# Linear attention with RMS norm and a mish FFN on one core: every engine in source order by slots, k^T v of all batches made in the first tile, q in whole rows

## The chip, the core and the metric

The kernel runs on one core of a Trainium2 chip. The metric is the device time of one execution in microseconds, lower is better. The core has a matrix engine (TensorE, PE in the profile), a vector engine (VectorE, DVE), a scalar engine (ScalarE, ACT), a general one (GpSimd, POOL) and a queue that issues transfers (SyncE, SP). Each works through its own list of instructions in order and waits on semaphores for the others; sixteen DMA engines move data between DRAM and the on-chip memory.

## The reference

Inputs are q, k, v of 8 batches, 8 heads, 576 tokens and 64 channels, a gain g of 64 channels, and two weight matrices, which arrive as 64-bit floats.

```python
kv = einsum('bhsd,bhse->bhde', k, v)          # 64x64 per batch and head
out = einsum('bhsd,bhde->bhse', q, kv)
rms = sqrt(mean(out * out, axis=-1, keepdims=True) + 1e-06)
x = (out / rms * g).transpose(0, 2, 1, 3).reshape(4608, 512)
h = x @ w_in                                  # 512 -> 2048
sp = where(h > 20, h, log1p(exp(minimum(h, 20))))
result = (h * tanh(sp)) @ w_out               # mish, 2048 -> 512
```

## The kernel before

The 4608 tokens are cut into nine tiles of 512. A tile crosses from one batch to the next (`segments`), since a batch has 576 tokens.

**Precision and Strassen.** Both large matmuls run on operands split in two (`split`: ACT rounds a copy to fp32r as the high half, DVE subtracts it to get the low half), and each product is three matmuls of halves. Each matmul is cut into 2x2 blocks by the Winograd form of Strassen's scheme: seven products (`PROD`) of sums of blocks, called A11, S1, S2, S4, A12, S3, A22 on the side of the tokens and T1 to T4, B11, B21, B22 on the side of the weights. The weights, 64-bit in DRAM, are first turned into 32-bit floats by a scaling on ACT and three integer operations on DVE (`join`), and then into the seven forms (`weight_forms`: `differences`, `first`, `rest`).

**The first stage** (tiles 0 to 8) makes h and mish(h) and stores them in DRAM (`gd`). Per tile four groups `n` of seven products run, each product 12 matmuls of 256 columns; this is a *slot*, so a tile is `NS` = 28 slots. Results are moved out of the accumulation banks by copies on ACT and additions on DVE (`group`, `put_in`), then mish runs on ACT. The bank "a" takes up A11, S2, S3 and, in the next group, A22; "bc" takes S1 with S4, and A12.

**Attention** for tile j is made during tile j-1, in two units of four heads (`unit_steps`): `load` of q in rows of 32 channels (128 bytes), `transpose` on DVE, `project` (k^T v times q on PE), `square` on ACT, `sums` (a matmul with a matrix of ones, which leaves the sum of squares on all rows of a head), `rstd` (a table load, Ln and Exp on ACT) and `normalize` on DVE. Tiles 0 and 1 use plain fp32, the others split halves. k^T v of batch j is made during tile j-1 as well: four loads (`kv_load`, two heads each, four DMAs, L206 and L207) and four products (`kv_product`, L242), which are copied into two block-diagonal tiles of halves, kvh and kvl. Then the seven forms of x are made (`x_sums`, `x_form`).

During tiles 1 to 8 the forms of w_out are made, 16 blocks one after the other, and stored in DRAM (`wod`).

**The second stage** multiplies mish(h) by w_out in 18 blocks of 256 tokens. The first is interleaved with the arrival of the weights (L673), the others run seven products of 24 matmuls each (L605).

**What sets the order.** A table `plan` holds for each slot what is recorded behind its product (`at`, `trace`). Only SP works in the order of the source (`manual_schedule(engines={SP})`); the instructions of PE, DVE, ACT and POOL are ordered by a scheduler that plans their times. The stores of gd are issued from ACT's queue.

Of the kernel before, what the change touches and what calls it, by code (L numbers as in the profile page):

```python
# [16 lines left out]


START = "w0 k0 q0 k1 q1 w1 c0 m0 t0 s0 m1 r0 t1 s1 c1 r1 w2 a0 f0 f1 a1 f2 f3 f4 f5 w3"


# [4 lines left out]
PROD = ((A11, B11, "a"), (S1, T1, "c"), (A22, T4, "p"), (S2, T2, "a"), (S4, B22, "c"), (A12, B21, "b"), (S3, T3, "a"))  # L26
# [3 lines left out]
def linear_attention_rms_mish_ffn(  # L30
# [26 lines left out]

    nc = tc.nc
# [4 lines left out]
    P = 128  # L63
    T = 512
# [5 lines left out]
    NQ = NF2 // 2  # L70
    G = 2 * P
# [10 lines left out]
    fp = ctx.enter_context(tc.tile_pool(name="fp", bufs=5))  # L82
# [5 lines left out]
    kvp = part1.enter_context(tc.tile_pool(name="kvp", bufs=1))  # L88
    xp = part1.enter_context(tc.tile_pool(name="xp", bufs=1))
    wst = part1.enter_context(ExitStack())  # L90
    wpools = {}

    def weight_pools(raw, x, forms):

        wst.close()
        for name, bufs in (("w64", raw), ("wx", x), ("wst", forms)):
            if bufs:
                wpools[name] = wst.enter_context(tc.tile_pool(name=name, bufs=bufs, reuse_waits="tile"))

    gcol = const.tile([P, 1], F32, name="gcol")  # L100
    ones = const.tile([P, P], F32R, name="ones")
    eps = const.tile([P, 1], F32, name="eps")
    gd = [tc.dram_tile([P, NFC, T], F32, name=f"gd{i}") for i in range(NT)]
    wod = [tc.dram_tile([P, 7, 2, G], F32, name=f"wod{c}") for c in range(NF2)]


    last = []

    def in_turn(i):
        if last:  # L110
            order = mybir.DependencyInfo(mybir.DependencyClass.NoSync, mybir.DependencyReason.DATA)
            tc.add_manual_dep(i.ins, last.pop().ins.name, order, reason="tables")
        last.append(i)

    def mish(o, i):
        in_turn(nc.scalar.activation(o, i, AF.Mish))  # L116
# [9 lines left out]
    def weight_forms(srcs, m, n, forms, put=None):  # L126
# [4 lines left out]
        def load():  # L131
            t = wpools["w64"].tile([P, 4, w, 2], U32, name="w64")
            n_ = 4 // len(srcs)
            for i, src in enumerate(srcs):
                dst = t[:, i].rearrange("p (m n) t -> p m (n t)", m=m) if n_ == 1 else t[:, n_ * i:n_ * i + n_].rearrange("p b n t -> p b (n t)")
                nc.sync.dma_start(dst, src)  # L136
            st["w"] = t.rearrange("p b n t -> p (b n) t")

        def scale():
            st["x"] = (wpools["wx"] if put else att).tile([P, 4 * w], F32, name="wx" if put else "fl")  # L140
# [9 lines left out]
        def differences():  # L150
            x = st["x"].rearrange("p (b n) -> p b n", b=4)
            d = st["w"].rearrange("p n t -> p (n t)").bitcast(F32)[:, 0:4 * w].rearrange("p (b n) -> p b n", b=4)
# [4 lines left out]
            st["f"] = forms()  # L157

        def parts(f0, f1, src):
            hi, lo = (st["f"][:, f0:f1, s].rearrange("p f m n -> p f (m n)") for s in range(2))  # L160
            split(hi, lo, src)

        def first():
            parts(T1, T4 + 1, st["d"])

        def rest():
            parts(B11, B11 + 1, st["x"][:, 0:1])
            parts(B21, B22 + 1, st["x"][:, 2:4])

# [3 lines left out]
        return load, scale, join, differences, first, rest, store  # L173
# [3 lines left out]
    def weight_in(j):  # L177
# [8 lines left out]
        return weight_forms(srcs, 2, P, forms)  # L186

    def weight_out(c, h):
        def forms():
            return wpools["wst"].tile([P, 7, 2, 1, P], F32R, name="wst")  # L190
# [7 lines left out]
        return weight_forms(srcs, 1, P, forms, store)  # L198


    def kv_load(b, h0, n, tiles):
        ts = []
        hs = slice(h0, h0 + n)
        for src in (k, v):
            m, r = tiles.pop(0), tiles.pop(0)
            nc.sync.dma_start(m, src[b, hs, 0:SM, :].rearrange("h (p c) d -> p h (c d)", c=CM))  # L206
            nc.sync.dma_start(r, src[b, hs, SM:S, :].rearrange("h p d -> p h d"))  # L207
# [3 lines left out]
    def kv_staging():  # L211
        ts = []
        for name in ("k", "v"):
            ts.append(kvp.tile([P, 2, CM * D], F32, name=f"{name}m"))
            ts.append(kvp.tile([SL, 2, D], F32, name=f"{name}r"))
        return ts

    kvf, kvh, kvl = {}, {}, {}  # L220

    def kv_new(b):
        def new(name, dtype):
            t = kvs.tile([P, NKC, P], dtype, name=name)
            nc.gpsimd.memset(t.bitcast(F32), 0.0)
            return t
        if b < T32:
            kvf[b] = new(("kvh0", "kvl0")[b], F32)
        if b >= T32 - 1:
            first = b < T32 + 1  # L230
            kvh[b] = new(f"kvh{b % 2}", F32R) if first else kvh[b - 2]
            kvl[b] = new(f"kvl{b % 2}", F32R) if first else kvl[b - 2]

    def kv_product(b, h0, nh, km, kr, vm, vr):
        ps = ps_t.tile([P, nh // 2, D], F32, name="s2")
        for i in range(nh // 2):
            for c in range(CM + 1):
                for o in range(2):
# [3 lines left out]
                    nc.tensor.matmul(ps[o * D:(o + 1) * D, i, :], kt, vt, start=(c == 0), stop=(c == CM))  # L242
        n = slice(h0 // 2, (h0 + nh) // 2)
        for r in (slice(0, D), slice(D, P)):
            if b < T32:
                nc.scalar.copy(kvf[b][r, n, r], ps[r, :, :])
            if b < T32 - 1:
                continue
            hi, lo = kvh[b][r, n, r], kvl[b][r, n, r]
            nc.scalar.copy(hi, ps[r, :, :])  # L250
            nc.vector.tensor_sub(lo, ps[r, :, :], hi.bitcast(F32))
# [11 lines left out]

    def unit_steps(j, u):
        st = {}

        def load(n):
            if n == 0:
                st["q"] = att.tile([P, 2, T], F32, name=f"qs{u}")
# [486 lines left out]
```

## Time and profile before

| | us |
|---|---|
| median of 3 runs | 930.96 |
| lowest, highest | 924.14, 932.98 |
| the profiled execution | 938.03 |
| its span, first to last instruction | 936.2 |

All views are of the profiled execution. Busy times are sums over an engine's instructions; a wait is put down to the instruction that ended it. "SPq" and "ACTq" are the queues that issue transfers. "PEclk" is the clock that TensorE was granted, 1.00 being full speed. The boundaries between tiles are taken from the first copy that follows a tile's first product (L374).

### The profile page before, as it was taken

How to read it: one execution, taken by the hardware profiler on the slowest of the kernel's cores; microseconds unless marked ns; L12 is line 12 of the kernel's file. 1: busy time of each engine (PE TensorE's matmuls, PEld its weight loads, DVE VectorE, ACT ScalarE, POOL GpSimd, SP SyncE). 2: the span in 40 equal slices, each digit the busy share in tenths (PEclk: the TensorE clock that was granted, in tenths of full speed). 3: DMA queues.
4: the chain of work that ended last, by engine and by line, in shares of the span. 5: the costliest groups of instructions: out<-in, count | busy, mean ns of one | idle time of the engine just before them, and what ended most of it. 6: DMA issues, size and time to landing. Idle time of an engine off the chain costs nothing.

```text
span 936.2 us, 17021 instructions
## 1 busy us (share of the span) xinstructions
PE 849.1 (91%) x6940; PEld 816.1 (87%) x6940; DVE 597.0 (64%) x832; ACT 512.8 (55%) x776; POOL 3.6 (0%) x14
## 2 busy tenths in 40 slices
PE   2687799898996998979899899999999999999997
PEld 1376699798896988969899898999999999999997
DVE  3676785665656557465753827767777767776661
ACT  2564767677676667666766744444444444444441
POOL 1000000000000000000000000000000000000000
PEclk9887889999897998999999999999999999999999
DMA  8565566676767667677741899443333443433421
GB/s 185 160 155 158 150 191 189 179 221 164 225 196 200 180 164 224 173 203 206 195 139 66 288 398 419 144 146 114 135 113 116 164 148 114 135 113 113 158 68 46
DMA packets 218861, 160.50 MB, mean 171 GB/s; under 512 B 91808, under 2 KB 208544, under 8 KB 217760
## 3 DMA queue, kind: packets, MB, share of 16 engines
q1 hardware_dynamic: 194016, 121.67, 44.3%
q10 hardware_dynamic: 24768, 37.76, 11.5%
q8 instruction: 54, 0.88, 0.4%
q14 instruction: 23, 0.19, 0.1%
HBM read 97.52 MB, written 61.87 MB: 170 GB/s over the span
## 4 chain that ended last, share of the span: by engine, by line
PE 70%; DMA 12%; SPq 6%; ACT 6%; DVE 3%; issue 2%; ACTq 0%; DVEq 0%
PE a L605 21%; PE bc L605 16%; PE a L411 16%; PE bc L411 11%; DMA w<-in_moe_w_out_dram 5%; SPq L274 3%; DMA w<-in_moe_w_in_dram 2%; SPq L136 2%; PE s L242 2%; PE q L673 2%; DMA qs<-in_q_dram 1%; DMA wod<-wst 1%; ACT L116 1%; ACT gf L119 1%; PE x L302 1%
## 5 line engine op out<-in xcount | busy, mean ns | idle before, releaser
L411 PE MATMUL a<-gf,wf 128*128 128x256 f32 x1728 | 248.1, 297 | 38.7 <-ACT ulb L116 22.3
L411 PEld LDWEIGHTS a<-gf,wf 128*128 128x128 f32 x1728 | 231.2, 202 | 47.1 <-ACT ulb L116 24.0
L605 PE MATMUL a<-wf,gf 128*128 128x256 f32 x1632 | 202.5, 283 | 2.3 <-ACT ur L374 1.3
L605 PEld LDWEIGHTS a<-wf,gf 128*128 128x128 f32 x1632 | 198.6, 192 | 2.9 <-ACT ur L374 1.5
L411 PE MATMUL bc<-gf,wf 128*128 128x256 f32 x1296 | 185.3, 292 | 8.4 <-ACT ur L379 3.8
L411 PEld LDWEIGHTS bc<-gf,wf 128*128 128x128 f32 x1296 | 171.7, 198 | 12.6 <-ACT ur L379 4.2
L605 PE MATMUL bc<-wf,gf 128*128 128x256 f32 x1224 | 152.8, 283 | 1.7 <-DVE gf L120 1.7
L605 PEld LDWEIGHTS bc<-wf,gf 128*128 128x128 f32 x1224 | 149.4, 192 | 1.9 <-DVE gf L120 1.9
L120 DVE TENSOR_TENSOR gf<-g,gf 128x1024 fp32r<-128x1024 f32 (+1 forms) x100 | 109.5, 1104 | 63.2 <-ACT gf L119 62.8
L119 ACT CAST gf<-g 128x1024 fp32r<-128x1024 f32 (+1 forms) x100 | 94.7, 955 | 58.9 <-PE bc L605 52.4
L119 ACT CAST gf<-s 128x1024 fp32r<-128x1024 f32 (+2 forms) x58 | 49.4, 851 | 39.3 <-PE a L605 28.0
L120 DVE TENSOR_TENSOR gf<-s,gf 128x1024 fp32r<-128x1024 f32 (+2 forms) x58 | 56.4, 973 | 17.4 <-ACT gf L119 17.2
L431 DVE TENSOR_TENSOR ur<-bc,ur 128x512 f32<-128x512 f32 x36 | 24.8, 688 | 44.8 <-PE bc L411 34.7
L388 ACT COPY ur<-a 128x512 f32<-128x512 f32 (+1 forms) x53 | 27.4, 517 | 35.2 <-PE a L605 26.0
L379 ACT COPY ur<-bc 128x512 f32<-128x512 f32 (+1 forms) x53 | 27.4, 517 | 35.2 <-PE bc L605 24.3
L120 DVE TENSOR_TENSOR fl<-fa,fh 128x1024 fp32r<-128x1024 f32 x28 | 34.2, 1222 | 14.6 <-ACT fh L119 14.3
L431 DVE TENSOR_TENSOR ur<-a,ur 128x512 f32<-128x512 f32 x36 | 24.8, 689 | 28.1 <-PE a L411 28.0
L116 ACT ACTIVATE ur<-ur 128x1024 f32<-128x1024 f32 x36 | 37.9, 1053 | 7.6 <-DVE ur L431 7.0
L120 DVE TENSOR_TENSOR gf<-gf 128x512 fp32r<-128x512 f32 x45 | 30.6, 689 | 6.3 <-ACT gf L119 6.2
L431 DVE TENSOR_TENSOR ula<-bc,ula 128x512 f32<-128x512 f32 x36 | 24.7, 687 | 12.5 <-PE bc L411 9.9
L308 ACT ACTIVATE fa<-x 128x1024 f32<-128x1024 f32 x18 | 18.4, 1025 | 25.2 <-PE x L304 18.8
L120 DVE TENSOR_TENSOR wst<-w,wst 128x512 fp32r<-128x512 f32 x16 | 11.0, 691 | 32.3 <-ACT wst L119 32.2
(103 smaller groups left out, 853.5 us busy)
## 6 DMA issues: line engine op xcount, KB each, us to landing
g<-gd SPq DMA_DIRECT2D x18, 2048.0 KB, 8.8
gd<-ur ACTq DMA_DIRECT2D x36, 512.0 KB, 4.4
wod<-wst SPq DMA_DIRECT2D x16, 896.0 KB, 5.6
wf<-wod SPq DMA_DIRECT2D x8, 1792.0 KB, 11.5
gd<-ula ACTq DMA_DIRECT2D x36, 256.0 KB, 3.5
gd<-ulb ACTq DMA_DIRECT2D x36, 256.0 KB, 3.9
out_dram<-ur SPq DMA_DIRECT2D x18, 512.0 KB, 2.8
w<-in_moe_w_in_dram SPq DMA_DIRECT2D x32, 256.0 KB, 4.4
```

What stands on the lines that cost most here:

```text
L116: in_turn(nc.scalar.activation(o, i, AF.Mish))
L119: nc.scalar.copy(hi, src)
L120: nc.vector.tensor_sub(lo, src, hi.bitcast(F32))
L136: nc.sync.dma_start(dst, src)
L242: nc.tensor.matmul(ps[o * D:(o + 1) * D, i, :], kt, vt, start=(c == 0), stop=(c == CM))
L274: nc.sync.dma_start(st["q"][32 * i:32 * i + 32, a, cols].rearrange("p (c d) -> p c d", d=32), q[b, h, s0:s0 + n_, d0:d0 + 32].rearrange("( ...
L379: nc.scalar.copy(dst(st, "22"), st["c"])
L388: nc.scalar.copy(dst(st, "12"), st["a"])
L411: nc.tensor.matmul(bank[:, jj], w[:, right, a, kc, :], xf[:, b, kc, :], start=first and jj == kc == s == 0, stop=(kc == 1 and s == 2), ski ...
L431: nc.vector.tensor_add(o, bank, o)
L605: nc.tensor.matmul(bank, gf[:, a, c, :], wo[c][:, right, b, :], start=first and c == s == 0, stop=(c == NF2 - 1 and s == 2), skip_group_ch ...
L673: nc.tensor.matmul(banks[b][:, h], gf[:, a, c, :], wo[2 * n + c][:, right, d, :], start=n == c == s == h == 0, stop=last_one, skip_group_c ...
```

## The change

All engines now follow the source (`manual_schedule(engines=None)`). A slot has a fixed form: first the evictions of the product before, then the product, then what the plan holds.

```diff
-    ctx.enter_context(tc.manual_schedule(engines={mybir.EngineType.SP}))
+    ctx.enter_context(tc.manual_schedule(engines=None))
+    def then(t, f):
+        evict.setdefault(t, []).append(f)
+    def slot(t, product=None):
+        for f in evict.pop(t, ()):
+            f()
+        if product:
+            product()
+        for f in plan.pop(t, ()):
+            f()
```

The order of the products S4 and A12 is swapped (in `PROD` and in the forms, `MADE`), S4 is formed in place, and mish runs one slot after the addition before it. The stores of gd are issued from SP instead of ACT's queue.

k^T v of batches 1 to 7 is made in tile 0, 28 products of two heads with two staging buffers, and kept in DRAM as plain fp32; a tile fetches the batch that it needs and splits it whole.

```diff
+    for n in range(len(order_kv) + len(staged)):
+        t = n * 6 // 8
+        at(t, lambda t=t: kv_next_product(t))
+        at(t, kv_next_load)
+    def kv_fetch(b):
+        raw[b] = kvs.tile([P, NKC, P], F32, name="kvr")
+        nc.sync.dma_start(raw[b], kvd[b])
+    def kv_split(b):
+        kvt[b] = kvs.tile([P, 2, NKC, P], F32R, name=f"kv{b % 2}")
+        split(kvt[b][:, 0], kvt[b][:, 1], raw[b])
```

q is loaded in runs of consecutive tokens: each of 32 rows takes a run of whole tokens (up to 4 KB), once for the lower and once for the upper 32 channels, so that q is read twice. The tokens of a tile stand in another order than before, and `o_store` puts them back with two or more DMAs per block.

```diff
+                        src = bass.AP(src.tensor, src.offset, [[R, 2], [run, R], [1, run - R]])
+                        dst = t[o * D:(o + 1) * D, a, c0:c0 + run - R]
+                        nc.sync.dma_start(dst, src)
```

The rms factors are made once per tile from tile 1 on: a matmul with a selector of eight columns collects the sums of squares of all heads in eight rows, one Ln and one Exp run on them, and the factors go through DRAM to be spread over the rows of each head. Until then x is scaled by g alone.

```diff
+                e = sel[:, 2 * u + a, :]
+                    nc.tensor.matmul(ss[j], e, st["sl"][:, a], start=u == a == 0, stop=False)
+                    nc.tensor.matmul(ss[j], e, st["sh"][:, a], start=False, stop=u == a == 1)
...
+        def keep():
+            nc.sync.dma_start(rd[j], st["r"])
+        def spread():
+            t = st["rr"] = att.tile([P, 2, T], F32, name="fa" if u else "fh")
+            for o in range(2):
+                src = rd[j][4 * u:4 * u + 4].rearrange("(a o) t -> o a t", o=2)[o]
+                nc.sync.dma_start(t[o * D:(o + 1) * D], src.partition_broadcast(D))
...
+                nc.vector.tensor_mul(o, o, st["rr"])
```

The steps of tile j's attention stand at fixed slots of tile j-1: the transposes at 0 and 7, the projections at 3 and 11, the sums at 8 and 15, `rstd` at 16, `keep` at 18, `spread` at 20, the multiplications at 23 and 24, the forms at 24 to 32. In the start, k and v of batch 0 are loaded through ACT's queue, and the weights' differences get a tile of their own.

**PE in tile 0.** Before, one product of k^T v (L242; km, vm are 512 tokens of k and v, kr, vr the last 64) stands among many slots (L411):

```order
L411 MATMUL a_319<-gf_110,wf_261 128x256 x6
L411 MATMUL bc_370<-gf_109,wf_175 128x256 x5
L411 MATMUL bc_370<-gf_109,wf_261 128x256 x6
L242 MATMUL s2_440<-vm_393,km_391 64x64 x8
L242 MATMUL s2_440<-vr_394,kr_392 64x64 x2
L411 MATMUL bc_587<-gf_108,wf_388 128x256 x6
L411 MATMUL a_319<-gf_111,wf_175 128x256 x6
L411 MATMUL a_319<-gf_111,wf_261 128x256 x6
```

Now (L233 is k^T v, L480 the slot's product):

```order
L480 MATMUL a_341<-gf_310,wf_267 128x256 x6
L480 MATMUL a_341<-gf_310,wf_319 128x256 x6
L233 MATMUL s2_127<-vm_224,km_222 64x64 x8
L233 MATMUL s2_127<-vr_225,kr_223 64x64 x2
L233 MATMUL s2_127<-vm_232,km_230 64x64 x8
L233 MATMUL s2_127<-vr_233,kr_231 64x64 x2
L480 MATMUL bc_407<-gf_310,wf_267 128x256 x6
L480 MATMUL bc_407<-gf_310,wf_319 128x256 x6
L233 MATMUL s2_127<-vm_370,km_368 64x64 x8
L233 MATMUL s2_127<-vr_371,kr_369 64x64 x2
```

One or two products of k^T v now follow nearly every slot of the first 21.

**SP in tile 0.** Before, between two blocks of w_in (L136) stand one load of k and v and pieces of q (L274):

```order
L136 DMA w64_625<-in_moe_w_in_dram 128x2x256 x4
L206 DMA km_674<-in_k_dram 128x2x256
L207 DMA kr_675<-in_k_dram 64x2x64
L206 DMA vm_676<-in_v_dram 128x2x256
L207 DMA vr_677<-in_v_dram 64x2x64
L274 DMA qs0_488<-in_q_dram 32x4x32
L274 DMA qs0_488<-in_q_dram 32x12x32
L136 DMA w64_719<-in_moe_w_in_dram 128x2x256 x4
```

Now (L135 is w_in, L212 and L213 are k and v, L503 a store of gd, L248 the store of a batch's k^T v):

```order
L135 DMA w64_711<-in_moe_w_in_dram 128x2x256 x4
L212 DMA km_726<-in_k_dram 128x2x256
L213 DMA kr_727<-in_k_dram 64x2x64
L212 DMA vm_728<-in_v_dram 128x2x256
L213 DMA vr_729<-in_v_dram 64x2x64
L212 DMA km_764<-in_k_dram 128x2x256
L213 DMA kr_765<-in_k_dram 64x2x64
L212 DMA vm_766<-in_v_dram 128x2x256
L213 DMA vr_767<-in_v_dram 64x2x64
L503 DMA gd0_91<-ula_405 128x2x256
L248 DMA kvd2_110<-kv1_129 128x512
L212 DMA km_808<-in_k_dram 128x2x256
```

Several loads follow one another, and the stores of gd stand behind them in the same queue.

**DVE at the end of a tile.** Before, in tile 1 (L332 is `normalize` of a unit, L287 the transpose of the next tile's q, L153 to L155 the differences of a block of w_out, L353 and L354 sums, L251 the low half of k^T v, L120 a low half):

```order
L332 SCALAR_TENSOR_TENSOR gf_107<-x2_1449,gcol_85,fa_1545 128x1024
L154 TENSOR_TENSOR w64_1549<-wx_1979,w64_1549 128x128
L353 TENSOR_TENSOR s1_1586<-gf_107 128x512
L287 STREAM_TRANSPOSE fa_1834<-qs0_1194 128x1024
L155 TENSOR_TENSOR w64_1549<-wx_1979,w64_1549 128x128
L354 TENSOR_TENSOR gf_107<-gf_107 128x2x256
L251 TENSOR_TENSOR kvl1_343<-s2_1741,kvh1_341 64x64
L120 TENSOR_TENSOR gf_108<-s1_1586,gf_108 128x512
```

Now, at the same place (L384 is the multiplication by the rms factors, L401, L402 and L404 the sums, L119 a low half, L500 an eviction):

```order
L384 TENSOR_TENSOR gf_131<-gf_131,fh_1904 128x1024
L384 TENSOR_TENSOR gf_131<-gf_131,fa_1907 128x1024
L119 TENSOR_TENSOR gf_310<-gf_131,gf_310 128x512
L401 TENSOR_TENSOR s1_132<-gf_131 128x512
L402 TENSOR_TENSOR gf_131<-gf_131 128x2x256
L119 TENSOR_TENSOR gf_310<-s1_132,gf_310 128x512
L500 TENSOR_TENSOR ula_1925<-bc_1979,ula_1925 128x512
L500 TENSOR_TENSOR ur_1942<-bc_1927,ur_1942 128x2x256
L500 TENSOR_TENSOR ur_1942<-a_1911,ur_1942 128x2x256
L404 TENSOR_TENSOR gf_131<-s1_132,gf_131 128x2x256
L119 TENSOR_TENSOR gf_331<-gf_131,gf_331 128x512
L293 STREAM_TRANSPOSE fa_2041<-qs_1697 128x1024
```

Both units are multiplied one after the other at the end of the tile, the evictions of the last slots stand behind the forms S1, and the transpose comes after the form S2.

592 lines of the change are left out of this document (337 added, 255 removed).

## The prediction

> **What bounds the kernel now.** I read the page's engine line first, then a table of windows by stage, the chain of waits, and the timeline of SP's queue. TensorE (PE) is busy for 91% of the span; VectorE (DVE) and ScalarE (ACT) are well below.
>
> ```profile
> PE 849.1 (91%) x6940; PEld 816.1 (87%) x6940; DVE 597.0 (64%) x832; ACT 512.8 (55%) x776; POOL 3.6 (0%) x14
> ```
>
> The average hides the stages. The windows below are: start, first tile, tiles 1 to 7, tile 8, the first 256 rows of the second matmul, its other 17 blocks, the end. The columns are length, busy time of each engine with its instructions, granted clock, DMA share, GB/s.
>
> ```profile
> core 0: us, PE busy (x) PEld busy (x) DVE busy (x) ACT busy (x) POOL busy (x), PEclk, DMA share, GB/s
> 0.00:36.00 36.00, 15.05 (x92) 7.47 (x93) 14.14 (x17) 11.90 (x16) 2.53 (x12) 0.94 0.76 183
> 36.00:126.60 90.60, 68.65 (x446) 59.50 (x445) 68.59 (x103) 57.08 (x91) 1.06 (x2) 0.80 0.62 168
> 126.60:523.90 397.30, 361.80 (x3064) 347.49 (x3063) 240.58 (x407) 273.89 (x427) 0.00 (x0) 0.96 0.64 182
> 523.90:565.50 41.60, 41.02 (x334) 40.10 (x334) 21.62 (x49) 21.95 (x47) 0.00 (x0) 1.00 0.94 366
> 593.60:932.00 338.40, 337.44 (x2808) 337.06 (x2808) 236.18 (x233) 138.17 (x182) 0.00 (x0) 1.00 0.36 121
> ```
>
> From 593.6 us on PE has no gaps, so nothing can be won there. The chain of waits gives its pace:
>
> ```profile
> 602.95 5.76 PE a L605 x48
> ```
>
> That is 0.12 us for a matmul of 256 columns. A tile of the first matmul is 28 slots of 12 such matmuls, 1.44 us each, 40.3 us in all. Attention adds, in columns, 12 times 512 for q and 8 times 512 for the sums of squares: 10,240 columns, 4.8 us. So a tile from 1 to 7 needs 45.1 us of PE without k^T v. The third row gives 56.8 us per tile. What lies between is k^T v and waiting. Tile 8, with neither, already runs at its floor. So the money lies in tiles 1 to 7, and the danger in tile 0, which takes over the k^T v of seven batches.
>
> **The change part by part.** *k^T v into the first tile.* What one step costs on PE and on SP's queue:
>
> ```profile
> 49.50 1.12 PE L242 MATMUL s<-vm,km 128*64 128x64 f32 x16 [2.15 <-DMA qs<-in_q_dram]
> 50.55 0.48 PE L242 MATMUL s<-vr,kr 64*64 64x64 f32 x4
> 60.49 0.69 PE L242 MATMUL s<-vm,km 128*64 128x64 f32 x16
> 61.10 0.33 PE L242 MATMUL s<-vr,kr 64*64 64x64 f32 x4
> ```
>
> ```profile
> 71.16 0.43 SPq L206 DMA_DIRECT2D km<-in_k_dram  x1
> 71.69 0.61 SPq L207 DMA_DIRECT2D kr<-in_k_dram  x1
> 72.36 0.59 SPq L206 DMA_DIRECT2D vm<-in_v_dram  x1
> 72.99 0.61 SPq L207 DMA_DIRECT2D vr<-in_v_dram  x1
> 74.81 1.95 SPq L136 DMA_DIRECT2D w<-in_moe_w_in_dram  x4
> ```
>
> ```profile
> L274 SPq DMA_DIRECT2D qs<-in_q_dram x256: 311/468/2191, 6.7 to 459.4; - x128
> L434 ACTq DMA_DIRECT2D gd<-ula x36: 366/367/590, 61.5 to 564.2; - x36
> ```
>
> Two heads are one product of 1.02 us at full clock (0.69 + 0.33), 1.60 at half clock, and one load of four DMAs, which takes SP 2.45 us to issue (71.16 to 73.60). Before, four products stand in each tile, so tiles 1 to 7 give up about 3.8 us of PE each. Now 26 loads stand in tile 0. SP issues there: 26 loads at 2.45 = 63.7; five weight blocks at 1.95 = 9.8; three q loads of 8 DMAs at 0.468 = 11.2; some 16 stores and fetches at 0.367 = 5.9. Sum 90.6 us, or 3.48 per load, if SP never waits. It does wait: the staging has two buffers, so load n+2 is queued behind the end of product n, and everything later on SP (weights, q, stores of gd) behind it. How long a load takes to land:
>
> ```profile
> km<-in_k_dram SPq DMA_DIRECT2D x28, 256.0 KB, 3.2
> vm<-in_v_dram SPq DMA_DIRECT2D x28, 256.0 KB, 4.0
> vr<-in_v_dram SPq DMA_DIRECT2D x28, 32.0 KB, 3.7
> w<-in_moe_w_out_dram SPq DMA_DIRECT2D x32, 256.0 KB, 6.0
> gd<-ula ACTq DMA_DIRECT2D x36, 256.0 KB, 3.5
> ```
>
> The last DMA of a load lands 3.7 us after its issue began, 3.1 after it ended. Then comes the product, 1.02, and in about half the cases a slot's product before it, 0.72 on average. So two loads take 3.1 + 1.02 + 0.72 + 2.45 = 7.3 us, 3.64 each. Both limits act on one queue in fixed order, so I take 3.75, a little above each. The unknown has two ends. Below: SP's bare 2.45, if all else slips in between. Above: landing as slow as the weights' 6.0 (5.4 after the issue), products and half a slot at half clock (1.60, 1.44): (5.4 + 1.60 + 1.44 + 2.45)/2 = 5.45. The middle value is nearest to the rows of the same loads, so it stands.
>
> [...]
>
> *The start.* k and v of batch 0 go to ACT's queue, q in rows of up to 4 KB instead of 128 bytes; the conversion of two weight blocks and both units still stand ahead of the first product on DVE and ACT. Before, the first product waits for weights:
>
> ```profile
> 8.91 1.12 ACT L141 ACTIVATE fl<-w 128x1024 f32<-128x1024 f32 x1 [6.90 <-DMA w<-in_moe_w_in_dram]
> 45.70 1.65 PE L411 MATMUL a<-gf,wf 128*128 128x256 f32 x6 [4.68 <-DVE wf L120]
> ```
>
> It ends at 47. The first weights landed at 8.91 anyway and the work behind them is the same, so I keep 47; ends 42 and 52. From there: 26 loads at 3.75 = 97.5, landing and product of the last 4.1, slots 21 to 27 10.1. Tile 1 starts at 158.7 instead of 126.6, **32 us lost**.
>
> *Tiles 1 to 7.* The instructions that come, go or shrink:
>
> ```profile
> L327 ACT ACTIVATE fa<-s,eps 128x1024 f32<-128x1024 f32 x18 | 20.1, 1114 | 17.9 <-PE s L319 9.2 <-PE s L322 8.8
> L328 ACT ACTIVATE fa<-fa 128x1024 f32<-128x1024 f32 x18 | 19.1, 1060 | 0.4
> L326 ACT ACT_TABLE_LOAD x18 | 23.1, 1283 | 1.0 <-PEq L740 0.7
> L250 ACT CAST kvh<-s 64x64 fp32r<-64x64 f32 x56 | 11.5, 206 | 6.8 <-DVE kvl L251 3.9 <-PE s L242 1.9 <-ACT ula L116 0.4
> L332 DVE SCALAR_TENSOR_TENSOR gf<-x,gcol,fa 128x1024 f32<-128x1024 f32 x18 | 23.0, 1280 | 11.2 <-ACT fa L328 7.3 <-PE s L242 3.9
> L251 DVE TENSOR_TENSOR kvl<-s,kvh 64x64 fp32r<-64x64 f32 x56 | 12.3, 220 | 17.3 <-ACT kvh L250 16.2
> L120 DVE TENSOR_TENSOR fl<-fa,fh 128x1024 fp32r<-128x1024 f32 x28 | 34.2, 1222 | 14.6 <-ACT fh L119 14.3
> L287 DVE STREAM_TRANSPOSE fa<-qs 128x1024 f32<-128x1024 f32 x14 | 17.4, 1243 | 0.6 <-DMA qs<-in_q_dram 0.4
> L353 DVE TENSOR_TENSOR s<-gf 128x512 f32<-128x512 f32 x9 | 6.2, 685 | 0.0
> L120 DVE TENSOR_TENSOR gf<-gf 128x512 fp32r<-128x512 f32 x45 | 30.6, 689 | 6.3 <-ACT gf L119 6.2
> PEld a L411 <- ACT ulb L116: 24.0, 9, 5.5
> ```
>
> ACT has 273.9/7 = 39.1 us per tile. Two pairs of Ln and Exp (2 times 2.17) become one on 512 columns, about 1.2: -3.1. Four table loads (L326's two and mish's two reloads behind them) become two: -2.6. Eight copies of 0.206 become one split of some 0.6: -1.0. That leaves 32.4 us. DVE has 240.6/7 = 34.4. Scaling by g stays near the 1.28 of L332, and two multiplications of 1.22 are added; eight 0.220 go, one 0.689 comes: 35.8. Both fit in 45.1, so they set no floor of their own. The wait of the last row, PE behind a late mish, should shrink, as evictions now lead each slot. What is late next is the end of a tile: from the first multiplication by the rms factors to the low half of the next q, DVE has 2 x 1.22, ten times 0.69 (four sums and forms in order, three evictions), 1.24 and 1.22: 11.8 us, and it waits for ACT's high halves, some 1.7. PE's slots 23 to 30 offer 11.5. That is 2.0 us late, 0.6 more on average for a block of w_out that falls there (1.8 us in a third of tiles), and about 1 for the second unit: 3.5 us per tile. Ends: 0, since both engines have room, and 7.9, what a tile loses now (56.8 - 45.1 - 3.8). The factors' way through DRAM is one store, 3.5 us by the row of gd<-ula against two slots (2.9), then four loads, 4 x 0.468 + 3.5 = 5.4 against three slots (4.3): up to 1.7 us late, but DVE arrives there late itself, and the 3.5 take it in. SP's other issues, some 42 per tile at about half a microsecond, fit twice in the tile. The doubled bytes of q run beside a DMA share of 0.64 and cost nothing; without that cover q would be late at the transpose. Tiles 1 to 7: 7 x (45.1 + 3.5) = 340 instead of 397.3, **57 won**.
>
> *The rest.* Tile 8 stays at 41.6, and 370.7 follow after 565.5: the swapped product, S4 formed in place and stores split by segment stand under PE's gapless 338.4; without that cover the split stores cost a few issues of half a microsecond. Sum: 158.7 + 340 + 41.6 + 370.7 = 911 against a span of 936.2. The profiled execution took 938.03, its span and 1.8 around it, while the median of the runs is 930.96, 0.75% lower. So (911 + 1.8) x 0.9925 = 906.
>
> **The rivals.** *Tile 0 chokes (slower).* If small DMAs crowd the engines, a load takes 5.45 us, tile 1 starts at 203, and the whole is 955, as a median 950. It decides from 4.7 us per load on, where the 57 won are used up. For it: the first tile moved 168 GB/s at a share of 0.62, 271 at a full one, and tile 0 now has about 29 MB (15.3 of k and v, 5.2 weights, 3.1 q, the rest stores), 107 us of full share. Against it: the 128-byte rows of q, which made that rate low, are gone, and tile 8 moved 366 GB/s at 0.94. [...] *Source order couples the engines.* Any late instruction holds its whole queue; if tiles keep losing 7.9 us, the sum is 942, as a median 937: no change. For it: DVE is 79% filled in fixed order. Against it: two slots of slack for each eviction. *The burst is hidden.* At 2.45 us per load tile 1 starts at 125, and the median is 872. For it: SP may run ahead of PE; against it: two staging buffers.
>
> **How the numbers follow.** Chances: the forecast 0.58, choking 0.15, coupling 0.13, hidden burst 0.14. The forecast's own range, from 3.3 to 4.2 us per load and 2 to 5.5 us per tile, is 889 to 924. The range that leaves out the choking case and the edge of the hidden burst is 873 to 937. One per cent, about what a measurement of this kernel can tell from no change, is 9.3 us: faster 0.72 (forecast and hidden burst), same 0.13 (coupling), slower 0.15 (choking).
>
> **What would show it.** Right: a first tile of 105 to 120 us with SP's queue issuing without pause and PE waiting for vr or vm; then tiles of 47 to 50 us with hardly any wait for mish; two table loads per tile; DVE above 70% there; PE still gapless in the second matmul. Wrong: tile 0 above 135 or below 95 us, or tiles above 52 us with PE behind DVE's low halves or behind the rms factors.

## The result, and the profile after

The changed kernel is slower by more than a quarter. The ratio is formed from runs of both kernels on the same chip.

| | before | after |
|---|---|---|
| median of the runs, us | 931.29 (4 runs, 924.14 to 932.98) | 1191.23 (4 runs, 1191.13 to 1194.02) |
| ratio, 95% interval | | 1.2817 (1.2748 to 1.2886) |
| the profiled execution, us | 938.03 | 1194.02 |
| its span, us | 936.2 | 1192.0 |
| mean granted clock | 0.962 | 0.877 |

For the stages I use one marker that both kernels have: the copy on ACT that moves out the first product of a tile (ula<-a, 128x512). "Start" runs to that copy of tile 0, and "rest" from that of tile 8 to the end of the span. In the changed order this copy can stand later behind its product than before, by up to ten us at the start, so that much at a border can belong to either side of it.

| us | start | tile 0 | tiles 1 to 7 | rest | span |
|---|---|---|---|---|---|
| before | 40.1 | 87.9 | 397.3 | 410.8 | 936.2 |
| after | 91.7 | 167.9 | 510.9 | 421.4 | 1192.0 |
| difference | +51.6 | +80.0 | +113.6 | +10.6 | +255.8 |

All stages of the first half lost. Here are the engine line and the clock and DMA rows (40 equal slices) of the page after.

```profile
PE 885.9 (74%) x6940; PEld 838.2 (70%) x6940; DVE 611.5 (51%) x801; ACT 464.6 (39%) x703; POOL 3.4 (0%) x19
PEclk9875696788797878978888788999999999999999
DMA  5223384752643435436352463599444434343531
```

PE runs the same 6940 matmuls, but it stands idle for a quarter of the span, and the work itself takes 37 us longer, at a granted clock that is lower in most slices with gaps. The DMA row falls to 2 and 3 again and again in the first half, while everybody waits. For what, the table of waits says (waiter, releaser: total us, times, longest).

```profile
ACT ur L448 <- DMA gd<-ur: 156.1, 15, 14.3
DVE fa L293 <- DMA qs<-in_q_dram: 72.2, 7, 12.5
PE x L319 <- ACT fh L118: 59.6, 7, 11.7
PE s L233 <- DMA vm<-in_v_dram: 54.9, 12, 21.5
PE bc L480 <- ACT ur L448: 54.6, 7, 9.0
```

The second row is late q. The third follows from it: PE's projection (L319) waits for what comes behind DVE's transpose. The first and the last are a late store: the copies of S1 (L448) wait for a buffer whose way to DRAM is not done, and PE waits for them. The fourth, the loads of k and v in tile 0, has a cause of its own in part, since 35.0 us of it stay in the repaired kernel below. One of the seven tiles in the timeline (start, length, engine, work, idle before it and its releaser):

```profile
284.90 1.25 DVE L293 STREAM_TRANSPOSE fa<-qs 128x1024 f32<-128x1024 f32 x1 [10.38 <-DMA qs<-in_q_dram]
286.18 11.22 SPq L288 DMA_DIRECT2D qs<-in_q_dram  x8
287.39 0.47 PE L319 MATMUL x<-fh,kv 128*128 128x128 f32 x1 [8.12 <-ACT fh L118]
...
300.56 6.90 SPq L506 DMA_DIRECT2D gd<-ur  x1
...
312.34 0.59 ACT L448 COPY ur<-bc 128x512 f32<-128x512 f32 x1 [13.89 <-DMA gd<-ur]
312.98 2.93 PE L480 MATMUL bc<-gf,wf 128*128 128x256 f32 x12 [9.00 <-ACT ur L448]
```

Eight DMAs of q keep SP for 11.2 us. A store behind them keeps it for 6.9, where such an issue took 0.34 before (the median of gd<-ur, on ACT's queue). The store that ACT waits for lands only at 312.3, and ACT and then PE stand still. Four windows of 5 us from the same stretch show what the DMA engines did (columns as in the prediction's windows):

```profile
285.00:290.00 5.00, 1.82 (x6) 1.63 (x7) 3.55 (x4) 2.51 (x4) 0.00 (x0) 0.50 0.11 30
290.00:295.00 5.00, 5.00 (x27) 5.00 (x26) 1.82 (x2) 2.48 (x3) 0.00 (x0) 0.59 0.14 52
295.00:300.00 5.00, 5.00 (x41) 4.50 (x40) 1.88 (x3) 1.53 (x2) 0.00 (x0) 1.00 0.15 54
300.00:305.00 5.00, 3.98 (x34) 3.77 (x32) 0.00 (x0) 0.00 (x0) 0.00 (x0) 1.00 0.64 212
```

With q in the queue the share is 0.14 to 0.15 and the rate 52 to 54 GB/s, although work is waiting. Two engines of sixteen are a share of 0.125. The source pattern of the new q load has a first dimension of 2 (the lower and the upper 32 channels), where before it had 32.

The Trainium skill has a rule for this, which the prediction overlooked. Its page "DMA: Bandwidth & Descriptors", section "Why a DMA increments its semaphore by 16 and not by 1", says that a transfer runs on the largest number of engines up to 16 that divides the slowest dimension (the outermost one other than 1) of both access patterns, and that SP's queue takes the lowest-numbered ones. By that rule q runs on two engines, always the same two; the windows agree (0.14 to 0.15 beside 0.125).

The trace does not name the engine of a packet, but it has the start, length and size of each, so one can count how many are in flight. Eight sizes, 384 to 3968 bytes, belong to this load of q alone. In the kernel after, these 8192 packets are in flight for 383 us, two at a time for 336 of them and never more than four. With the load cut in two (the first experiment) the same packets take 119 us, up to 19 at a time. The 512-byte packets, which are those of the stores of w_out's forms (wod), show how a store comes late: from 301 to 304 some 14 of them are in flight beside two of q, then until 307.5 almost only two of q, and only then the last of the store, two at a time beside other transfers, to 310.5. So a share of that store waited for q.

### The profile page after: what moved, and what is told of

Read it like the earlier page. It is cut to its first block, busy times and chain, and to the rows that moved or that the text cites. A ratio compares the mean times of both kernels' runs of the same rounds, so it can differ in the third digit from the quotient of the medians.

```text
span 1192.0 us, 16959 instructions
## 1 busy us (share of the span) xinstructions
PE 885.9 (74%) x6940; PEld 838.2 (70%) x6940; DVE 611.5 (51%) x801; ACT 464.6 (39%) x703; POOL 3.4 (0%) x19
## 5 line engine op out<-in xcount | busy, mean ns | idle before, releaser
L480 PE MATMUL bc<-gf,wf 128*128 128x256 f32 x1296 | 192.3, 306 | 61.2 <-ACT ur L448 54.6
L480 PEld LDWEIGHTS bc<-gf,wf 128*128 128x128 f32 x1296 | 181.4, 212 | 65.1 <-ACT ur L448 56.1
L480 PE MATMUL a<-gf,wf 128*128 128x256 f32 x1296 | 183.5, 299 | 27.0 <-ACT ur L457 13.9
L480 PEld LDWEIGHTS a<-gf,wf 128*128 128x128 f32 x1296 | 173.2, 205 | 31.8 <-ACT ur L457 16.2
L119 DVE TENSOR_TENSOR gf<-g,gf 128x1024 fp32r<-128x1024 f32 (+1 forms) x123 | 132.9, 1087 | 87.9 <-ACT gf L118 87.8
L118 ACT CAST gf<-g 128x1024 fp32r<-128x1024 f32 (+1 forms) x123 | 114.5, 939 | 90.2 <-DVE g L708 65.1
L448 ACT COPY ur<-bc 128x512 f32<-128x512 f32 (+1 forms) x53 | 27.4, 517 | 186.0 <-DMA gd<-ur 156.1
L233 PE MATMUL s<-vm,km 128*64 128x64 f32 x448 | 24.2, 265 | 81.6 <-DMA vm<-in_v_dram 54.9
L233 PEld LDWEIGHTS s<-vm,km 128*64 128x64 f32 x448 | 20.1, 172 | 86.3 <-DMA vm<-in_v_dram 28.6
L319 PE MATMUL x<-fh,kv 128*128 128x128 f32 (+7 forms) x52 | 21.3, 409 | 59.6 <-ACT fh L118 59.6
L480 PEld LDWEIGHTS a<-a,wf 128*128 128x128 f32 x432 | 56.5, 196 | 9.8 <-DVE ur L500 5.6
L480 PE MATMUL a<-a,wf 128*128 128x256 f32 x432 | 60.1, 290 | 2.5 <-DVE ur L500 2.4
L319 PEld LDWEIGHTS x<-fh,kv 128*128 128x128 f32 x52 | 13.2, 254 | 61.5 <-ACT fh L118 61.0
L293 DVE STREAM_TRANSPOSE fa<-qs 128x1024 f32<-128x1024 f32 x14 | 17.4, 1242 | 72.2 <-DMA qs<-in_q_dram 72.2
L500 DVE TENSOR_TENSOR ula<-bc,ula 128x512 f32<-128x512 f32 x36 | 24.7, 685 | 35.5 <-PE bc L480 23.3
L500 DVE TENSOR_TENSOR ur<-bc,ur 128x512 f32<-128x512 f32 x36 | 24.6, 683 | 35.0 <-PE bc L480 23.9
L118 ACT CAST gf<-gf 128x512 fp32r<-128x512 f32 x45 | 27.7, 617 | 37.6 <-DVE gf L406 18.2
```

Of the source, the lines that this page charges most:

```text
L118: nc.scalar.copy(hi, src)
L119: nc.vector.tensor_sub(lo, src, hi.bitcast(F32))
L233: nc.tensor.matmul(kvps[o * D:(o + 1) * D, b % 2, h0 // 2 + i, :], kt, vt, start=(c == 0), stop=(c == CM))
L293: nc.vector.transpose(t.rearrange("p a (c d) -> p (a c) d", d=R), src)
L319: nc.tensor.matmul(ps[:, c], kl, qh, start=True, stop=False)
L448: then(t + 2, lambda: nc.scalar.copy(dst(st, "22"), st["c"]))
```

## The experiments

Three theories stood against each other at first; the expectations call them A, B and C. A, the form: q moves on two engines, and all else follows. B, the order: source order, the burst in tile 0 and SP's single queue cost the time, and q is only seen waiting. C: the doubled bytes of q cost it. The stages of all runs with a table row are counted as above; the medians are in the text, the spans belong to the profiled execution.

| us | start | tile 0 | tiles 1 to 7 | rest | span |
|---|---|---|---|---|---|
| q cut in two | 60.8 | 129.4 | 366.9 | 421.6 | 978.7 |
| q and output cut | 62.1 | 128.7 | 370.8 | 418.5 | 980.1 |
| before, q on two engines | 71.7 | 126.9 | 577.2 | 419.3 | 1195.1 |
| before, q cut | 40.4 | 79.1 | 380.9 | 416.8 | 917.2 |
| scheduler back | 45.0 | 133.0 | 367.3 | 412.2 | 957.6 |
| v from ACT's queue | 63.6 | 128.3 | 370.0 | 418.7 | 980.6 |
| three buffers | 61.0 | 127.0 | 367.2 | 418.5 | 973.8 |
| q from GpSimd's queue | 68.5 | 115.0 | 357.3 | 418.9 | 959.7 |
| factors earlier | 60.8 | 132.2 | 360.0 | 418.6 | 971.6 |
| the last three together | 60.2 | 111.4 | 347.7 | 418.8 | 938.2 |
| before, q cut, from GpSimd's queue | 38.3 | 74.0 | 395.8 | 420.0 | 928.2 |

### The q load cut in two

Each q load becomes two DMAs of 32 rows. Bytes and packets stay the same; the first dimension of the pattern is 32 instead of 2, and SP issues twice as many DMAs.

```diff
-                        src = bass.AP(src.tensor, src.offset, [[R, 2], [run, R], [1, run - R]])
-                        dst = t[o * D:(o + 1) * D, a, c0:c0 + run - R]
-                        nc.sync.dma_start(dst, src)
+                        for e in range(2):
+                            half = bass.AP(src.tensor, src.offset + e * R, [[run, R], [1, run - R]])
+                            dst = t[o * D + e * R:o * D + (e + 1) * R, a, c0:c0 + run - R]
+                            nc.sync.dma_start(dst, half)
```

> The changed kernel, but each q transfer is cut into its two halves of 32 rows: same bytes, same packets of up to 4 KB, twice as many issues on SP. Theory A (a transfer whose slowest dimension is 2 runs on two of the sixteen DMA engines, so that 18.9 MB of q crawl): 885 to 925 us, about 910, with waits for q below 10 us in total. Theory B (the burst of k and v in tile 0 and SP's single queue cost the time): 1150 to 1220 us, since SP issues more than before. Theory C (the doubled bytes of q cost it): 1170 to 1210 us, nothing changes.

The median is 982.14 us, ratio to the kernel before 1.0571 (1.0531 to 1.0611). Of the 255.8 us that the span had grown by, 213.3 are gone (1192.0 to 978.7): 30.9 in the start, 38.5 in tile 0, 144.0 in tiles 1 to 7, none in the rest. Theories B and C expected no gain and are out as the cause of the large loss. But A had expected 885 to 925 us: what is left, 42.5 us of span, has other causes.

### A dose of four, which was none

To see the time grow with the number of engines, the 32 rows were written as four times eight.

```diff
-                            half = bass.AP(src.tensor, src.offset + e * R, [[run, R], [1, run - R]])
+                            half = bass.AP(src.tensor, src.offset + e * R, [[8 * run, 4], [run, 8], [1, run - R]])
```

> As the run before, but the 32 rows are written as 4 times 8, so that the slowest dimension is 4. Theory A: if the transfer keeps that form, four engines carry q and the time lies between, 930 to 1050 us; if the form is folded back to 32, it is that of the run before. Theories B and C: no difference to the run before.

One run took 982.94 us, the same as the form with 32. Its trace has the same 8192 packets of q, in flight for 123 us and up to 19 at a time, as with the form of 32: rows at one distance written as two dimensions seem to be folded into one. The run decides nothing on four engines.

### Only q changed in the kernel before, on two engines and on sixteen

The kernel before keeps its scheduler, its k^T v per tile and its rms factors per unit. It gets the q load in whole rows with the tokens in the new order, the matching output stores, one buffer for q (so that the second unit's q comes later in the start), and loads at other slots of the plan. The first version uses the pattern of the change, the second cuts q and output stores into DMAs of 32 rows. The cut diffs below show q's lines and the slots only.

```diff
-                st["q"][32 * i:32 * i + 32, a, cols].rearrange("p (c d) -> p c d", d=32),
-                q[b, h, s0:s0 + n_, d0:d0 + 32].rearrange("(c p) d -> p c d", p=32),
+                src = bass.AP(src.tensor, src.offset, [[32, 2], [run, 32], [1, run - 32]])
+                nc.sync.dma_start(st["q"][o * D:(o + 1) * D, a, c0:c0 + run - 32], src)
...
-                at(max(t - (15 if u else 24) + 3 * n, n // 2 - 1), lambda u=u, n=n: units[j][u][0](n))
+                at(t + 4 if u else max(t - 14, 0), lambda u=u, n=n: units[j][u][0](n))
```

```diff
-                src = bass.AP(src.tensor, src.offset, [[32, 2], [run, 32], [1, run - 32]])
-                nc.sync.dma_start(st["q"][o * D:(o + 1) * D, a, c0:c0 + run - 32], src)
+                src = bass.AP(src.tensor, src.offset + e * 32, [[run, 32], [1, run - 32]])
+                nc.sync.dma_start(st["q"][32 * i:32 * i + 32, a, c0:c0 + run - 32], src)
```

> The kernel before with nothing changed but q in whole rows by transfers whose slowest dimension is 2, and the output put back in order; k^T v stays spread over the tiles, and the scheduler orders all engines but SP. Theory A: 1050 to 1250 us, most of the loss of the change. Theory B: 925 to 950 us. Theory C: 925 to 960 us.

> The kernel before with q in whole rows by transfers of 32 rows each and the output put back in pieces of 32 rows; k^T v spread over the tiles, rms factors per unit, the scheduler for all engines but SP. Theory A (the form of two engines is what made whole rows slow): 905 to 940 us, against 1197 with the form of two. If whole rows are slow in any form: above 1000.

On two engines: 1196.89 us in one run, as slow as the whole change, without source order and without the burst. Its table of waits has another victim, since stores of gd go out from ACT's queue there; now the forms of w_out wait for their store:

```profile
ACT wst L119 <- DMA wod<-wst: 128.4, 9, 19.9
```

On sixteen: 914.52 us, ratio 0.985 (0.9787 to 0.9913), 1.5% faster than the kernel before and faster than the changed one. The windows row of its tiles 1 to 7:

```profile
119.00:500.00 381.00, 358.78 (x3050) 345.21 (x3049) 236.87 (x405) 268.64 (x424) 0.00 (x0) 0.97 0.70 209
```

That is 54.4 us per tile instead of 56.8. So the form of the transfers is worth 282 us in this kernel alone (some 3 of them by the output stores, as the next run shows), theory B is not needed for the large loss, and q in whole rows gains if it is spread. Which of its parts gains (fewer packets, other slots, the buffer) was not taken apart.

### The output stores cut as well

The last stores have at most four blocks as their slowest dimension. They too were cut into DMAs of 32 rows, on top of the cut q. This kernel, called the repaired one below, is the base of the next runs.

```diff
-                    dst = bass.AP(dst.tensor, dst.offset, [[DM, hi - lo], [L * DM, R], [1, DM]])
-                    src = st["o"][(lo - c0) * R:(hi - c0) * R, r, :]
-                    nc.sync.dma_start(dst, src)
+                    for c in range(hi - lo):
+                        dst = out[row + c:row + c + 1, :]
+                        dst = bass.AP(dst.tensor, dst.offset, [[L * DM, R], [1, DM]])
+                        src = st["o"][(lo - c0 + c) * R:(lo - c0 + c + 1) * R, r, :]
+                        nc.sync.dma_start(dst, src)
```

> The q transfers cut in halves, and the stores of the output, whose slowest dimension is at most 4, cut into pieces of 32 rows. Theory A: 3 us less than with the q transfers alone, at the end of the span, where the last store stands bare (6.9 us after the last copy in the changed kernel, 3.8 in the one before). Theories B and C: no difference, or a little slower by the issues added.

980.22 us, ratio 1.054 (1.0505 to 1.0575). The rest is 3.1 us shorter (421.6 to 418.5), nearly all of it at the very end, as expected: after the last copy the kernel of the change ran 7.2 us on (1184.76 to 1192.0), this one 4.4 (975.75 to 980.1), the kernel before 4.1 (932.07 to 936.2). The medians differ by less than their spread, so the whole time does not show it.

### The scheduler back on all engines but SP

```diff
-    ctx.enter_context(tc.manual_schedule(engines=None))
+    ctx.enter_context(tc.manual_schedule(engines={mybir.EngineType.SP}))
```

> The changed kernel with q and output transfers on all engines (980 us), but ordered by the scheduler as before, all engines but SP. If the fixed order couples the engines and costs the 31 us by which tiles 1 to 7 miss the forecast: 930 to 960 us. If the order isn't the cause: 970 to 990.

955.84 us, ratio 1.0267 (1.0189 to 1.0346). It wins 17.1 us in the start and 6.3 in the rest; tile 0 is 4.3 longer, tiles 1 to 7 are 3.5 shorter. The time lies in the range expected for a coupling in tiles 1 to 7, but by luck: little of the gain is there. The timelines of the start, first of the repaired kernel, then of this one, show what source order cost:

```profile
49.71 2.90 PE L481 MATMUL a<-gf,wf 128*128 128x256 f32 x12 [10.92 <-DVE gf L383]
...
62.09 0.58 ACT L444 COPY ula<-a 128x512 f32<-128x512 f32 x1
```

```profile
41.83 2.93 PE L481 MATMUL a<-gf,wf 128*128 128x256 f32 x12
...
45.02 0.58 ACT L444 COPY ula<-a 128x512 f32<-128x512 f32 x1
```

The first product is 8 us earlier, and its copy follows at once instead of 9.5 us later behind conversions and splits that wait for DVE. So source order costs in the start and at tile 8, and little in tiles 1 to 7.

### What holds tile 0 of the repaired kernel: three runs on SP's queue

SP's queue in tile 0 of the repaired kernel:

```profile
73.97 8.81 SPq L289 DMA_DIRECT2D qs<-in_q_dram  x16
82.88 0.38 SPq L212 DMA_DIRECT2D km<-in_k_dram  x1
...
121.87 9.09 SPq L289 DMA_DIRECT2D qs<-in_q_dram  x16
131.33 0.35 SPq L507 DMA_DIRECT2D gd<-ur  x1
131.79 0.39 SPq L212 DMA_DIRECT2D km<-in_k_dram  x1
```

And PE, for which the load behind the second q block came late:

```profile
136.84 1.12 PE L233 MATMUL s<-vm,km 128*64 128x64 f32 x16 [10.31 <-DMA vm<-in_v_dram]
```

From 73.97 to 134.4 SP issues almost without pause, and only twelve loads of k and v get out, 5.0 us each. One unit's q costs 9 us of issuing, more than three loads of k and v. Three edits follow from it: v from ACT's queue; a third buffer for km and vm, with the small parts issued behind both large ones; q from GpSimd's queue.

```diff
+            e_ = nc.scalar if src is v else eng
-            eng.dma_start(m, src[b, hs, 0:SM, :].rearrange("h (p c) d -> p h (c d)", c=CM))
+            e_.dma_start(m, src[b, hs, 0:SM, :].rearrange("h (p c) d -> p h (c d)", c=CM))
```

> The changed kernel with q and output transfers on all engines (980 us), and v issued from ACT's queue, k from SP's: SP issues 52 DMAs fewer in tile 0. If SP's issuing sets tile 0's pace: a first tile of 105 to 120 us instead of 139, 945 to 965 in all. If the two staging buffers and the landing set it: 130 to 140 us, 970 to 985 in all, or more, since ACT now waits for the buffers too.

```diff
...
-    open_pools(wst, ("w64", 1), ("wd", 1), ("kvp", 2))
+    open_pools(wst, ("w64", 1), ("wd", 1), ("kvp", 2), ("kvm", 3))
```

> The changed kernel with q and output transfers on all engines (980 us), with three staging buffers instead of two for the large parts of k and v, and the two small parts issued behind them. If the buffers set tile 0's pace: a first tile of 105 to 125 us, 950 to 970 in all. If SP's issuing sets it: 130 to 140 us, 970 to 985 in all.

```diff
-                            nc.sync.dma_start(dst, half)
+                            nc.gpsimd.dma_start(dst, half)
```

> The changed kernel with q and output transfers on all engines (980 us), and q issued from the queue of GpSimd, which is idle, instead of SP's: SP loses 48 issues, some 26 us, in tile 0, and nothing else changes. If SP's issuing sets tile 0's pace: a first tile of 100 to 115 us from first copy to first copy instead of 129, and 950 to 970 in all. If the buffers or the DMA engines set it: 125 to 132 us, 975 to 985 in all.

One run each: 982.34, 975.62 and 961.48 us. (The expectations of the first two start from a tile 0 of 139 us, and so count it from an earlier mark than the table, which has 128.7.) v from ACT's queue changed nothing in tile 0 (128.3), as expected if buffers and landing set the pace, but it is no clean test, since ACT works in source order and now waits for the buffers itself. A third buffer alone gives 1.7 us there, as expected if SP's issuing sets it. q off SP gives 13.7 in tile 0, as expected if SP's issuing counts, and 13.5 in tiles 1 to 7, and costs 6.4 in the start. SP's largest wait in that run, from 45 to 175 us:

```profile
SPq L212 <- PE s L233: 43.6, 15, 31.4
```

SP waits for the two buffers, but 31.4 us of it are one wait in the start. From 85 us on the row is 8.5 us, and in the repaired kernel it is 7.4 there. So the row doesn't show that the buffers take SP's place as the limit of tile 0.

### The rms factors fetched earlier

In tiles 1 to 7 of the repaired kernel two rows speak for the factors' way through DRAM: the wait of the whole run, and one tile of the timeline.

```profile
DVE gf L385 <- DMA fh<-rd: 17.6, 7, 4.6
```

```profile
448.69 1.23 DVE L385 TENSOR_TENSOR gf<-gf,fh 128x1024 f32<-128x1024 f32 x1 [4.58 <-DMA fh<-rd]
451.72 1.23 DVE L385 TENSOR_TENSOR gf<-gf,fa 128x1024 f32<-128x1024 f32 x1 [1.80 <-DMA fa<-rd]
...
459.05 2.90 PE L481 MATMUL bc<-gf,wf 128*128 128x256 f32 x12 [3.87 <-DVE ula L501]
```

The store moves from slot 18 to 17, the fetches from 20 to 18.

```diff
-        steps(1, 18, "keep")
-        steps(0, 20, "spread0")
+        steps(1, 17, "keep")
+        steps(0, 18, "spread0")
```

> The changed kernel with q and output transfers on all engines (980 us), and the rms factors stored one slot and spread two slots earlier. If DVE's wait for the factors' way through DRAM (18 us for the first loads over seven tiles) and what queues behind it on DVE cost the tiles their 31 us beyond the forecast: tiles 1 to 7 lose 10 to 20 us, 960 to 970 in all. If that wait is covered: 975 to 985.

973.34 us in one run, between the two ranges expected: tiles 1 to 7 are 10.8 us shorter (1.5 per tile), and tile 0 is 3.5 longer.

### Three edits together

Three buffers, q of tiles 1 to 8 from GpSimd's queue, and the factors earlier.

```diff
-                            nc.sync.dma_start(dst, half)
+                            (nc.gpsimd if j else nc.sync).dma_start(dst, half)
```

> The changed kernel with q and output transfers on all engines (980 us), q issued from GpSimd's queue from tile 1 on, three staging buffers for the large parts of k and v, and the rms factors spread two slots earlier. If SP's issuing and the two buffers together set tile 0's pace, each taking over when the other is lifted: a first tile of 95 to 108 us, tiles of 50 us, 930 to 950 in all. If something else stands behind both (landing, the weights' conversion): a first tile of 112 to 118 us as with GpSimd's queue alone, 950 to 960 in all.

940.61 us, ratio 1.0118 (1.0057 to 1.0179), still about 1% slower than the kernel before. Tiles 1 to 7 take 49.7 us each, and the time lies in the range expected if issuing and buffers together set tile 0's pace. But tile 0 itself takes 111.4 us, outside that expectation's 95 to 108 and just under the other's 112. Windows of tile 0 and of tiles 1 to 7:

```profile
55.00:165.00 110.00, 81.81 (x818) 67.44 (x819) 58.66 (x77) 45.69 (x72) 15.83 (x32) 0.80 0.92 260
```

```profile
172.00:519.00 347.00, 325.32 (x2556) 309.67 (x2555) 249.18 (x380) 225.38 (x356) 94.55 (x192) 1.00 0.69 212
```

The DMA share in tile 0 is 0.92 at 260 GB/s, so the DMA engines themselves may be what comes next there. That is argued, not shown: tile 8 of the kernel before moved 366 GB/s at 0.94, with other transfers.

PE's largest waits in tiles 1 to 7 of this kernel are for the low halves of the next q, 12.3 of some 21 us:

```profile
PE x L321 <- DVE fl L119: 7.2, 7, 1.5
PE ss L354 <- DVE fl L119: 5.1, 7, 1.7
```

### The faster kernel with q from GpSimd's queue

The edit that helped the repaired kernel was tried on the kernel that beat both.

```diff
-                    nc.sync.dma_start(st["q"][32 * i:32 * i + 32, a, c0:c0 + run - 32], src)
+                    (nc.gpsimd if j else nc.sync).dma_start(st["q"][32 * i:32 * i + 32, a, c0:c0 + run - 32], src)
```

> The kernel before with q in whole rows by transfers of 32 rows (914.5 us), and q issued from GpSimd's queue from tile 1 on. If SP's issuing still holds up tile 0 there: 900 to 910 us. If q is hidden in any queue once it uses all engines: 912 to 918.

931.81 us, ratio 1.0032 (0.9996 to 1.0067), so it loses what the other had won and lies above both ranges expected. Tile 0 is 5.1 us shorter, tiles 1 to 7 are 14.9 longer. GpSimd waits for q's single buffer:

```profile
POOL qs L278 <- DVE fa L288: 221.0, 11, 39.1
```

Why the tiles grow is open: that wait is idle time of an engine with nothing else to do. The best kernel remains the one at 914.52 us.

## Why the prediction was wrong

The spans side by side: forecast 911, after 1192.0, repaired 980.1, three edits together 938.2. The error of 281 us splits into 212 for the form of the transfers and 69 for what the repaired kernel still misses.

**The step that failed: "The doubled bytes of q run beside a DMA share of 0.64 and cost nothing".** The bytes were counted and the engines that carry them were not. The same sentence says what comes without that cover, and it came: q was late at the transpose, by 72.2 us in seven waits, and stores with it. The diff has the pattern, `[[R, 2], [run, R], [1, run - R]]`; 64 rows of up to 4 KB looked better than 128-byte pieces in every respect but the one that decided. Cutting the same transfers in two took 213 us back, and putting the same pattern into the kernel before cost 282 beside its cut form. That is shown in both directions. The output stores, which the prediction put under PE's gapless work, have the same form, at 3 us; what shows is at the very end, behind the last copy.

**The start, kept at 47.** The row quoted there (45.70) was not the first product; before, that ran at this time:

```profile
36.06 3.24 PE L411 MATMUL a<-gf,wf 128*128 128x256 f32 x12
```

After the change it ran at 79.39, behind q of the second unit:

```profile
60.97 1.25 DVE L293 STREAM_TRANSPOSE fh<-qs 128x1024 f32<-128x1024 f32 x1 [15.99 <-DMA qs<-in_q_dram]
...
79.39 2.90 PE L480 MATMUL a<-gf,wf 128*128 128x256 f32 x12 [10.92 <-DVE gf L382]
```

In the repaired kernel it ends at 52.6. The forecast's upper end was 52. What the forecast did not see is the copy behind it, 9.5 us late behind work that source order puts first. To the marker the start is 22 us longer than before, and the scheduler takes 17 of them back.

**Tile 0 at 3.75 us per load.** The forecast put the start of tile 1 at 158.7, a marker of about 160 (before, the marker stood 1.4 us behind it). The repaired kernel has it at 190.8, the three edits at 171.7. The loads came at 5.0 us each in the stretch from 73.97 to 134.4 instead of 3.75. The mechanism was right in kind: one queue in fixed order, and two buffers. The mis-sized term is q's issues. It had 3.7 us per unit (8 DMAs at 0.468); two halves take 9.0 (16 at 0.56), and the load that stands behind them starts late. With q on another queue the stage falls from 128.7 to 115.0, with all three edits to 111.4. The Trainium skill says in the page "DMA: Bandwidth & Descriptors", section "Issuing engines are not separate DMA queues", that issuing from several engines saves only the time to issue, and calls that usually small beside the DMA itself. Here the move was worth 14 us in tile 0 and as much in tiles 1 to 7. That all of it is time of issuing is not shown, since q got a queue of its own with it.

**Tiles 1 to 7 at 45.1 + 3.5 us.** In the kernel after they took 73.0 each, because of q's form. Repaired they take 53.0, with the three edits 49.7: 46.5 busy by the window above (325.32 of 347.00 us) and 3.1 idle. The stall of 3.5 was right in size once SP was free and the factors came earlier, and more than half of it stood where the prediction had put it, behind the low halves of the next q (12.3 us in seven tiles). In the repaired kernel "up to 1.7 us late, but DVE arrives there late itself, and the 3.5 take it in" failed: DVE waited up to 4.6 us there, and two slots earlier brought 1.5 us per tile. PE's own 45.1 was 1.4 too low.

**The rest, unchanged.** It grew by 8 us in the kernels in source order with cut output stores, and by 10.6 in the kernel after. Nearly all of the 8 is one place in tile 8, here in the repaired kernel:

```profile
582.34 1.05 SPq L683 DMA_DIRECT2D wf<-wod  x2
583.48 1.71 SPq L507 DMA_DIRECT2D gd<-ur  x1
592.53 0.59 ACT L449 COPY ur<-bc 128x512 f32<-128x512 f32 x1 [9.65 <-DMA gd<-ur]
...
593.17 2.93 PE L481 MATMUL bc<-gf,wf 128*128 128x256 f32 x12 [7.10 <-ACT ur L449]
```

A store of gd is issued behind the large fetches of the second stage's weights, and lands 9 us later. Before, these stores had ACT's queue. The prediction counted their issues in SP's sum and not whom they stand behind. With the scheduler the rest was 412.2, beside 410.8 before, although the stores stayed on SP's queue, so the queue alone does not cost the 8 us. Putting the stores back on ACT's queue alone was not tried. In the kernel before with q cut the rest grew too, by 6.0 us, at another place: PE waits 3.9 us for DVE at the beginning of the second matmul there, and 0.4 before.

**The rivals.** "Tile 0 chokes" had a place of the loss right and not its mechanism: it spoke of small DMAs that crowd sixteen engines, while in the kernel after most of them had nothing to do. Only with the three edits does the share reach 0.92, where that rival would begin. "Source order couples the engines" was wrong about the tiles (3.5 us of 370.8) and would have been right about the start. "The burst is hidden" never came near: the best tile 0 with the burst takes 111.4 us against 79.1 without it.

**The range.** The forecast's own range, 889 to 924, is narrower than its stated ends: 3.3 to 4.2 us per load and 2 to 5.5 per tile add up to spans of 889 to 937, as medians 884 to 932. The result is far outside either.

What the rest of the change is worth, all parts together, is seen in two kernels with cut q: the best with it 940.61, the best without it 914.52. Tiles 1 to 7 win 33 us (380.9 to 347.7), the start and tile 0 lose 52. The burst and the shared factors were not tried by themselves in the kernel before, so the gap is not their price alone: the two differ in the order of the engines, in the queues of the stores and of q, and in the staging buffers too.

## What to carry to other kernels

Before costing a rewritten transfer, read the slowest dimension of both its sides: longer rows and fewer packets were worth nothing here when a leading 2 put them on two engines, and stores that shared the queue with them were late too. A DMA share that stays at a simple fraction (0.14 beside 2/16) while engines wait for transfers is the sign to look for, and the count of packets in flight settles it. When work is gathered into one stage, add up the issue time of its queue with every DMA that the repair of another transfer brings.

## What the runs showed of the hardware

- While transfers with a leading dimension of 2 filled the queue, 52 to 54 GB/s were moved in all, and DMAs behind them on the same queue were held in issuing: 6.90 us for one store at 300.56, against 0.339 as the median before, on ACT's queue. SP's own 128 issues of q lay between 0.5 and 5.4 us:

```profile
L288 SPq DMA_DIRECT2D qs<-in_q_dram x128: 506/822/5422, 4.4 to 714.3; - x128
```

- Late data cost twice: PE's 6940 matmuls took 885.9 us at a mean clock of 0.877, and 842.2 us at 0.965 in the kernel with the three edits. In the tile shown above the granted clock was 0.59 in the window from 290 us, behind PE's 8 us of waiting, and 1.00 from 295 on.
- A pattern of four times eight equally spaced rows made packets of the same number and sizes, and took the same time within 0.1%, as one of 32 rows.
